# Two more weight subtractions on GpSimd for the last eight experts, and TensorE transposes for the last expert's tokens

## The chip, the cores and the metric

The kernel runs on one core of one Trainium2 chip. The metric is the device time of one execution in microseconds (us). Five engines work side by side on a core: TensorE (PE in the rows; PEld is its weight load), VectorE (DVE), ScalarE (ACT), GpSimd (POOL) and SyncE (SP), which here issues the weight loads. Each engine takes its own instructions in order, and they wait for one another through semaphores.

## The reference

Causal attention over 8 batches, 8 heads, 576 positions and 64 channels gives 4608 tokens of 512 values. A router then sends every token to one of 16 experts, and an expert is two matrix products:

```
for g in range(G):
    ...
    for e in range(Eg):
        ...
        h = np.maximum(xg[mask_e] @ w1[g, e], 0.0)
        ye = h @ w2[g, e]
        ...
        out[tok_idx] = combined[:, None] * ye
```

`w1` is 512 x 1024 and `w2` is 1024 x 512 for each expert, all in fp32.

## The kernel before

The first half of the time is attention and routing, which the change leaves alone. The second half (`moe`) works through 16 *slots*, one expert each, from the fullest to the emptiest; slot k takes up to `CAPS[k]` tokens, from 384 down to 256.

**Precision.** TensorE multiplies in a rounded fp32 form (`F32R`). Each operand is therefore split into a rounded high part and a low part, low = raw - high, and each product is done as high x high, high x low and low x high. Tokens give `xh`, `xl`; the hidden layer gives `hh`, `hl`; weights give `wh`, `wl`.

**Weights** (`Expert.load`, lines 970 to 1003). An expert has four blocks i = 0 to 3 (two halves of `w1`, two of `w2`), each 1 MB loaded by SP into one of three raw buffers, and each cut into four pieces j = 0 to 3 of 128 x 512. ScalarE casts every piece to its high part (line 991). The low part is made in one of two ways. For some pieces GpSimd subtracts (line 994). For the others ScalarE copies the piece a second time into a PSUM tile `pw` (line 999), and VectorE subtracts that from the raw piece (line 1000). The text below calls the pieces W0 to W15, piece W(4i+j) being piece j of block i. Before the change VectorE makes the low parts of W0, W4, W8, W10, W12 and W14, and GpSimd the ten others.

**Tokens** (`Slot.x_items`, lines 1034 to 1067). GpSimd gathers a slot's rows by indirect DMA (line 950). They must be turned so that channels lie on partitions. In slots 0 and 1 TensorE does that, with transposes into PSUM (line 1042), a ScalarE cast (1043) and a VectorE subtraction (1044) for each of four channel groups. In slots 2 to 15 VectorE does it with 32 stream transposes (line 1059) of 32 partitions each, 16 items of two; then ScalarE casts `xh` in two halves (1063) and VectorE subtracts `xl` in two halves (1064). With these widths the list holds eight transpose items of two and two split items, so a slot has 16 stream transposes.

**Products.** `h_items` makes the hidden layer in eight items of 12 matmuls (line 1092), each followed by a ScalarE Relu to `hh` (1087) and a VectorE `hl` (1088). `y_items` makes the second product in four items (line 1147, or line 1114 for the slots 14 and 15, whose `CAPS` is 256). For slots 1 to 13 the result comes out turned: ScalarE copies it to `yT` (1144, 1158), VectorE turns it back in 16 stream transposes during the *next* slot's hidden layer (1193), ScalarE scales the rows (1196), and GpSimd scatters them (955).

**Order** (lines 1407 to 1421). The order on TensorE, VectorE and ScalarE is written out by hand; GpSimd and SP are ordered by the planner. In slot k, after hidden item i come one item of the turning back of slot k-1 and weight piece W(i) of expert k+1. Ahead of second-product item i come four items of slot k+1's tokens, and weight pieces W(8+2i) and W(9+2i). Hence the eight transpose items run ahead of the first two second-product items, both splits ahead of the third, and the ScalarE queue after the splits is W12, W13, a `yT` copy, W14, W15, a `yT` copy, then the first Relu of slot k+1.

Of the kernel before, what the change touches and what calls it, by code (L numbers as in the profile page):

```python
# [24 lines left out]
E = 16  # L25
# [6 lines left out]

CAPS = [384, 368, 344, 332, 322, 314, 306, 300, 294, 288, 284, 280, 272, 264, 256, 256]
NL = 4
ROW = NTOK + P


# [16 lines left out]
def attn_moe(ctx, tc, qk, v, s, wr, w1, w2, out, stop_at=None, dbg=None):  # L54
# [8 lines left out]
    st.count = cst.tile([P, E], F32, name="count")  # L63
    st.lists = cst.tile([P, NV, E, NL], F32, name="lists")
    st.hot = cst.tile([P, B, NB, E], BF16, name="hot")
# [558 lines left out]
class Router:  # L624


    def __init__(self, tc, ac, sm, end, ps_t, ps_s, wr_f, wr_sb, xs, st):
# [25 lines left out]
        self.cols = iota("cols", [[1, P]])  # L653
        self.thr = iota("thr", [[P, NL + 1]])
        self.four = iota("four", [[1, NL]])
        self.lT = ac.tile([20, NB * P], F32, name="lT")
# [84 lines left out]
    def batch(self, b, xtail, xh, xl):  # L741
# [82 lines left out]
        place, us, pl = (small(i) for i in range(3))  # L824
        u4 = pc[:, 128:128 + NB * NL].rearrange("p (t h) -> p t h", h=NL)
        off = pc[:, 0:NB * E].rearrange("p (t e) -> p t e", e=E)
# [9 lines left out]

        U = [P, NB, NL]
        u = T("u", U[1:])
# [6 lines left out]
        yield  # L845
        col = T("col", [NB, E, NL], BF16)
        V.tensor_tensor(out=col, in0=ohb.unsqueeze(3).to_broadcast([P, NB, E, NL]),
# [73 lines left out]
def moe(tc, w1, w2, xs, st, out):  # L921
    nc = tc.nc
    V = nc.vector
    ident, mc = st.ident, st.cst
    with ExitStack() as ctx:
# [37 lines left out]
        class Expert:  # L963
# [6 lines left out]
            def load(self, hi=(None,) * 4, lo=(None,) * 4, eng=V):  # L970

                pieces = []

                with after(tc, *(loads[-1:] if 0 < self.u < E else ())):
                    e = nc.values_load(self.e, engines=[ENG.SP], min_val=0, max_val=E - 1)
                for i, w in enumerate((w1, w1, w2, w2)):

                    turn = 4 * self.u + i
                    q, n = (x1, 2) if turn % 3 < 2 else (x2, 1)
                    raw = q.tile([P, 4, 512], F32, name=f"raw{self.u}_{i}", tag="raw", bufs=n)  # L980
                    q, n = (wp, 4) if turn % 6 < 4 else (wq, 2)
                    h = q.tile([P, 4, 512], F32R, name=f"wh{self.u}_{i}", tag="wh", bufs=n)
                    l = q.tile([P, 4, 512], F32R, name=f"wl{self.u}_{i}", tag="wl", bufs=n)
                    self.h.append(h)
                    self.l.append(l)

                    def piece(j, i=i, w=w, raw=raw, h=h, l=l):
                        if j == 0:
                            loads.append(nc.sync.dma_start(raw, w[bass.ds(e, 1), i % 2].rearrange("o p a c -> p (o a) c")))
                        with after(tc, hi[i], lo[i]):  # L990
                            self.casts.append(nc.scalar.copy(h[:, j], raw[:, j]))  # L991

                            if j in ((1, 2, 3) if i < 2 else (1, 3)) or eng is not V:
                                self.low = nc.gpsimd.tensor_tensor(out=l[:, j], in0=raw[:, j],  # L994
                                                                   in1=h[:, j].bitcast(F32), op=ALU.subtract)
                                return

                            ps = pt.tile([P, 512], F32R, name=f"pw{self.u}_{i}_{j}", tag="pt")
                            nc.scalar.copy(ps, raw[:, j])
                            V.tensor_tensor(out=l[:, j], in0=raw[:, j], in1=ps.bitcast(F32), op=ALU.subtract)  # L1000

                    pieces += [lambda j=j, piece=piece: piece(j) for j in range(4)]
                return pieces
# [18 lines left out]
        class Slot:  # L1022
# [11 lines left out]
            def x_items(self):  # L1034
                u, cap = self.u, self.cap
                self.xh, self.xl = xhl(u, 0 if u == 0 else u + 1)

                def item(c):
                    q, tag = (pm[0], "pm") if u == 0 else (pt, "pt")
                    ps = q.tile([P, 512], F32, name=f"px{u}_{c}", tag=tag)  # L1040
                    for t, r in enumerate(self.rows):
                        nc.tensor.transpose(ps[:, t * P:t * P + r], self.xg[:r, t, c * P:(c + 1) * P], ident[:r, :r])
                    self.split = (nc.scalar.copy(self.xh[:, c, :cap], ps[:, :cap]),
                                  V.tensor_tensor(out=self.xl[:, c, :cap], in0=ps[:, :cap],
                                                  in1=self.xh[:, c, :cap].bitcast(F32), op=ALU.subtract))

                if u < 2:
                    return [lambda c=c: item(c) for c in range(4)]

                xt = turned(u)  # L1050
                nb = -(-cap // 32)

                def turn(j, i0):

                    n = len(range(j, nb, 4))
                    for i in (i0, i0 + 1):
                        src = self.xg[32 * j:32 * j + 32].rearrange("p t (c i n) -> p t c i n", c=4, n=32)
                        dst = xt[32 * i:32 * i + 32].rearrange("p c (t j n) -> p t c j n", j=4, n=32)
                        V.transpose(dst[:, 0:n, :, j], src[:, 0:n, :, i])  # L1059

                def split(a):
                    xh, xl, x = (t[:, a:a + 2, :cap] for t in (self.xh, self.xl, xt))
                    nc.scalar.copy(xh, x)  # L1063
                    V.tensor_tensor(out=xl, in0=x, in1=xh.bitcast(F32), op=ALU.subtract)  # L1064

                return ([lambda j=j, i=i: turn(j, i) for j in range(4) for i in (0, 2)] +
                        [lambda a=a: split(a) for a in (0, 2)])
# [191 lines left out]
        def run(items):  # L1259
            for f in items:  # L1260
                f()
# [15 lines left out]
        X = first.x_items()  # L1277
# [53 lines left out]
        with tc.manual_schedule(engines={ENG.PE}):  # L1331
# [10 lines left out]
            W = wts[1].load((first.rounded, rest.split[0], None, None), (None, rest.split[1], None, None))  # L1342
            run(W[:8])
            low = wts[1].low
            X, Z = slots[1].x_items(), first.z_items()
# [61 lines left out]
        Z = []  # L1407
        with tc.manual_schedule(engines={ENG.PE, ENG.DVE, ENG.Activation}):
            for k in range(1, E):
                W = wts[k + 1].load() if k + 1 < E else []  # L1410
                for i, f in enumerate(slots[k].h_items()):
                    f()
                    run(Z[i:i + 1] + W[i:i + 1])
                    if i == 4 and k + 2 < E:
                        slots[k + 2].gather()
                X = slots[k + 1].x_items() if k + 1 < E else []
                for i, f in enumerate(slots[k].y_items()):
                    run((Z[8:] if i == 0 else []) + X[4 * i:4 * i + 4] + W[8 + 2 * i:10 + 2 * i])
                    f()
                Z = slots[k].z_items()  # L1420
            run(Z)
# [164 lines left out]
```

## Time and profile before

| what | value |
|---|---|
| time, median of 3 runs | 954.95 us (954.18 to 956.15) |
| the profiled execution: its own time | 956.56 us |
| the profiled execution: span, first to last instruction | 954.8 us |
| PE busy | 875.1 us, 92% |
| DVE busy | 719.0 us, 75% |
| ACT busy | 615.3 us, 64% |
| POOL busy | 594.6 us, 62% |
| mean granted TensorE clock | 0.976 of full speed |

Times in the rows below are microseconds from the start of the span. A row of a timeline begins with the start and the duration; merged rows give the number of instructions as xN, and the bracket at the end is the idle time just before the row on that engine and what ended it. The shares of busy time are means over stages with different limits, so the stage that the change touches, from about 700 us to the end, is read by itself.

### The profile page before, as it was taken

The page shows a single profiled execution, that of the slowest core. Times are in us where ns is not written, and L with a number is a line of the kernel's source. Part 1 is how long each engine was busy: PE and PEld are TensorE (multiplying, and loading weights), DVE is VectorE, ACT ScalarE, POOL GpSimd, SP SyncE. Part 2 cuts the span into 40 slices and gives each one's busy share as a digit, 9 for nine tenths or more (in the row PEclk, how much of TensorE's full clock was granted, in tenths as well). Part 3 has the DMA queues.
Part 4 walks back from the last instruction along what each step waited for, and adds up shares of the span by engine and source line. Part 5 has one row for each costly group of instructions (what it writes and reads, how often), then busy time and mean ns, then how long its engine had stood idle before and what let it go on. Part 6 is the DMA issues. An engine that isn't in the chain of part 4 may idle for free. (4 is left out here: it accounts for less than half of the span.)

```text
span 954.8 us, 17985 instructions
## 1 busy us (share of the span) xinstructions
PE 875.1 (92%) x5640; PEld 785.2 (82%) x5640; DVE 719.0 (75%) x2032; ACT 615.3 (64%) x1396; POOL 594.6 (62%) x716
## 2 busy tenths in 40 slices
PE   4868999999999999998887999999999999999983
PEld 3657788887878788887686999999999999998882
DVE  7545586886868686876387578898888889988850
ACT  5546777776777677767634556667677666676640
POOL 9645666675757576534775447666676777676530
PEclk9999999999999999999898999999999999999987
DMA  6999988887888889723546345546555555565410
GB/s 184 217 182 207 240 217 214 194 224 197 222 197 224 210 213 231 174 69 112 194 142 211 130 160 189 186 162 225 182 204 187 201 194 176 209 221 210 143 42 22
DMA packets 80502, 174.66 MB, mean 183 GB/s; under 512 B 9580, under 2 KB 42988, under 8 KB 72208
## 3 DMA queue, kind: packets, MB, share of 16 engines
q1 hardware_dynamic: 70496, 153.52, 58.1%
q0 software_dynamic: 7488, 18.89, 5.6%
q10 hardware_dynamic: 2416, 1.03, 0.5%
q8 instruction: 47, 0.77, 0.3%
q14 instruction: 55, 0.45, 0.2%
HBM read 108.97 MB, written 19.69 MB: 135 GB/s over the span
## 5 line engine op out<-in xcount | busy, mean ns | idle before, releaser
L994 POOL TENSOR_TENSOR wl<-raw,wh 128x512 fp32r<-128x512 f32 x166 | 214.1, 1302 | 77.7 <-ACT wh L991 60.8
L221 DVE CUSTOM_DVE_ANT_0 mx<-pm,mask 128x192 bf16<-128x192 f32 (+4 forms) x320 | 129.4, 421 | 53.2 <-PE pm L213 49.0
L991 ACT CAST wh<-raw 128x512 fp32r<-128x512 f32 x256 | 155.2, 616 | 10.0 <-issue 9.4
L1092 PE MATMUL ph<-xh,wh 128*128 128x256 f32 (+13 forms) x512 | 145.9, 304 | 4.6 <-ACT xh L1063 3.9
L1092 PE MATMUL ph<-xl,wh 128*128 128x256 f32 (+13 forms) x512 | 146.4, 305 | 4.1 <-DVE xl L1064 3.8
L268 PE MATMUL ps<-WA 68*128 68x320 f32 (+4 forms) x384 | 136.9, 360 | 10.7 <-DMA WA<-tl 4.5
L213 PE MATMUL pm<-WA 66*128 66x288 f32 (+4 forms) x384 | 126.7, 359 | 17.6 <-DMA WA<-ch 10.3
L308 PE MATMUL po<-pt,VT 128*128 128x256 f32 (+3 forms) x512 | 123.2, 358 | 4.2 <-ACT sums L315 2.7
L1147 PE MATMUL py<-hl,wh 128*128 128x256 f32 (+13 forms) x448 | 113.6, 302 | 2.0 <-DVE hl L1088 2.0
L1147 PE MATMUL py<-hh,wh 128*128 128x256 f32 (+13 forms) x448 | 112.7, 301 | 0.0
L1059 DVE STREAM_TRANSPOSE xt<-xg 32x256 f32<-32x256 f32 (+1 forms) x224 | 109.5, 489 | 3.4
L270 PE MATMUL ps<-WB 128*128 128x320 f32 (+4 forms) x384 | 111.3, 303 | 0.0
L308 PE MATMUL po<-pu,VT 128*128 128x320 f32 (+1 forms) x384 | 107.8, 389 | 0.0
L1193 DVE STREAM_TRANSPOSE yr<-yT 32x384 f32<-32x384 f32 (+1 forms) x208 | 104.5, 502 | 4.2
L287 POOL TENSOR_SCALAR_AFFINE_SELECT pt<-pt 128x128 f32<-128x128 f32 (+2 forms) x192 | 63.9, 342 | 67.4 <-ACT pt L278 63.7
L1092 PEld LDWEIGHTS ph<-xl,wh 128*128 128x128 f32 x512 | 98.0, 191 | 7.8 <-DVE xl L1064 6.1
L1092 PEld LDWEIGHTS ph<-xh,wh 128*128 128x128 f32 x512 | 97.9, 191 | 7.2 <-ACT xh L1063 5.8
L308 PEld LDWEIGHTS po<-pt,VT 128*128 128x128 f32 x512 | 88.8, 195 | 18.1 <-issue 5.3
L213 PEld LDWEIGHTS pm<-WA 66*128 66x128 f32 (+1 forms) x384 | 69.8, 194 | 31.0 <-DVE mc L221 14.0
L370 POOL TENSOR_TENSOR xTl<-xT,xTh 128x512 fp32r<-128x512 f32 x30 | 38.2, 1273 | 90.6 <-ACT xTh L366 90.6
L1087 ACT ACTIVATE hh<-ph 128x256 fp32r<-128x256 f32 (+13 forms) x128 | 53.7, 420 | 62.7 <-PE ph L1092 61.9
L1092 PE MATMUL ph<-xh,wl 128*128 128x256 f32 (+13 forms) x512 | 90.8, 301 | 0.0
(245 smaller groups left out, 2017.5 us busy)
## 6 DMA issues: line engine op xcount, KB each, us to landing
raw<-in_w_dram SPq DMA_DIRECT2D x64, 1024.0 KB
r<-in_qk_dram SPq DMA_DIRECT2D x32, 576.0 KB
WA<-hl SPq DMA_DIRECT2D x61, 288.0 KB
WB<-hl SPq DMA_DIRECT2D x61, 288.0 KB
VT<-in_v_dram SPq DMA_DIRECT2D x32, 384.0 KB
WB<-hl SPq DMA_DIRECT2D x64, 144.0 KB
xs<-xr SPq DMA_DIRECT2D x15, 512.0 KB
WA<-cumd SPq DMA_DIRECT2D x56, 4.5 KB
```

The source lines that it names most:

```text
L213: nc.tensor.matmul(ps[:rows, :cw], WA[i][0:66, QA, h, QO + q0:QO + q0 + rows], WA[i][0:66, KA, h, QO + c0:QO + c0 + cw], start=True, stop= ...
L221: nc.vector.tensor_tensor_reduce(out=tmp[:rows, :cw], in0=ps[:rows, :cw], in1=mk[:rows], scale=1.0, scalar=-3.0e38 if c0 == 0 else mo, op0 ...
L268: nc.tensor.matmul(ps[:rows, o:o + w], WA[i][0:68, KA, h, QO + k0:QO + k0 + rows], WA[i][0:68, QA, h, QO + q0:QO + q0 + w], start=True, st ...
L270: nc.tensor.matmul(ps[:rows, o:o + w], WB[p % NBB][:, KA, h, k0:k0 + rows], WB[p % NBB][:, QA, h, q0:q0 + w], start=False, stop=True)
L287: nc.gpsimd.affine_select(out=d, in_=d, pattern=[[0, len(u)], [1, rows]], compare_op=ALU.is_ge, fill=0.0, base=0, channel_multiplier=-1)
L308: nc.tensor.matmul(po[0][:, qa - base:qb - base], VT[p % NVT].rearrange("p t a d -> p (t a d)")[:, (3 * t + 1 + h) * 64:][:, 0:P], x[:, c: ...
L991: self.casts.append(nc.scalar.copy(h[:, j], raw[:, j]))
L994: self.low = nc.gpsimd.tensor_tensor(out=l[:, j], in0=raw[:, j], in1=h[:, j].bitcast(F32), op=ALU.subtract)
L1059: V.transpose(dst[:, 0:n, :, j], src[:, 0:n, :, i])
L1092: self.product = nc.tensor.matmul(pss[f][:, :cap], w[f // 4][:, c, (f % 4) * P:(f % 4 + 1) * P], x[:, c, :cap], start=(c == 0 and w is sel ...
L1147: self.product = nc.tensor.matmul(pss[c][:, :cap], w[2 + f // 4][:, f % 4, c * P:(c + 1) * P], x[:, f, :cap], start=(f == 0 and w is self. ...
L1193: V.transpose(dst[:, 0:n, :, i], src[:, 0:n, :, j])
```

## The change

For experts 8 to 15 (`self.u >= LATE`), which are loaded during slots 7 to 14, the low parts of W10 and W14 are made by GpSimd instead of by the second ScalarE copy and the VectorE subtraction. For slot 15 the tokens are turned by TensorE as in slots 0 and 1: four items, each of two transposes, one cast and one subtraction, and one item stands ahead of each of slot 14's second-product items.

```
+LATE = 8
...
-                            if j in ((1, 2, 3) if i < 2 else (1, 3)) or eng is not V:
+                            if j in ((1, 2, 3) if i < 2 or self.u >= LATE else (1, 3)) or eng is not V:
                                 self.low = nc.gpsimd.tensor_tensor(out=l[:, j], in0=raw[:, j],
                                                                    in1=h[:, j].bitcast(F32), op=ALU.subtract)
                                 return
...
-                if u < 2:
+                if u < 2 or u == E - 1:
                     return [lambda c=c: item(c) for c in range(4)]
...
                 X = slots[k + 1].x_items() if k + 1 < E else []
+                n = 4 if len(X) > 4 else 1
                 for i, f in enumerate(slots[k].y_items()):
-                    run((Z[8:] if i == 0 else []) + X[4 * i:4 * i + 4] + W[8 + 2 * i:10 + 2 * i])
+                    run((Z[8:] if i == 0 else []) + X[n * i:n * i + n] + W[8 + 2 * i:10 + 2 * i])
                     f()
```

## Rows read from the trace of the kernel before

**Rows 1.** Busy time by stretch: length, busy us of each engine (instructions), clock, DMA.
```profile
858.00:884.00 26.00, 24.08 (x193) 23.39 (x193) 23.34 (x50) 17.99 (x40) 17.82 (x16) 1.00 0.56 202
...
900.00:920.00 20.00, 17.02 (x76) 14.49 (x76) 17.09 (x35) 10.61 (x21) 12.57 (x11) 0.83 0.21 83
```

**Rows 2.** Waits from 600 to 955 us: total us, times, longest us.
```profile
PE ph L1092 <- ACT xh L1063: 3.9, 5, 2.2
PE ph L1092 <- DVE xl L1064: 3.8, 9, 0.8
```

**Rows 3.** Waits of VectorE from 700 to 912.6 us.
```profile
DVE hl L1088 <- ACT hh L1087: 3.7, 8, 0.5
```

**Rows 4.** Timeline of VectorE in slots 13 and 14.
```profile
866.47 0.43 DVE L1088 SCALAR_TENSOR_TENSOR hl<-ph,hh 128x264 fp32r<-128x264 f32 x1 [0.44 <-ACT hh L1087]
...
884.77 2.25 DVE L1059 STREAM_TRANSPOSE xt<-xg 32x256 f32<-32x256 f32 x5
...
904.75 3.58 DVE L1059 STREAM_TRANSPOSE xt<-xg 32x256 f32<-32x256 f32 x8
```

**Rows 5.** Timeline of ScalarE: three late slots' token casts, and the queue behind them.
```profile
727.41 1.27 ACT L1063 CAST xh<-xt 128x588 fp32r<-128x588 f32 x2 [3.28 <-DVE xt L1059]
...
861.30 1.17 ACT L1063 CAST xh<-xt 128x528 fp32r<-128x528 f32 x2 [2.79 <-DVE xt L1059]
...
866.05 0.39 ACT L1087 ACTIVATE hh<-ph 128x264 fp32r<-128x264 f32 x1
...
887.04 1.14 ACT L1063 CAST xh<-xt 128x512 fp32r<-128x512 f32 x2 [2.26 <-DVE xt L1059]
...
890.44 0.58 ACT L999 CAST pw<-raw 128x512 fp32r<-128x512 f32 x1
890.96 0.62 ACT L991 CAST wh<-raw 128x512 fp32r<-128x512 f32 x1
...
912.67 1.14 ACT L1063 CAST xh<-xt 128x512 fp32r<-128x512 f32 x2 [2.80 <-DVE xt L1059]
```

**Rows 6.** Timeline of TensorE in slots 14 and 15.
```profile
887.72 0.39 PE L1092 MATMUL ph<-xh,wh 128*128 128x256 f32 x1 [0.36 <-ACT xh L1063]
...
900.05 0.40 PE L1114 MATMUL py<-wh,hh 128*128 128x512 f32 x1
...
910.73 0.39 PE L1114 MATMUL py<-wh,hl 128*128 128x512 f32 x1
913.35 0.58 PE L1092 MATMUL ph<-xh,wh 128*128 128x256 f32 x1 [2.23 <-ACT xh L1063]
...
927.11 0.28 PE L1092 MATMUL ph<-xh,wh 128*128 128x256 f32 x1
...
928.55 0.40 PE L1114 MATMUL py<-wh,hh 128*128 128x512 f32 x1
```

**Rows 7.** Instruction groups from 560 to 955 us: busy us, mean ns of one, idle before.
```profile
L994 POOL TENSOR_TENSOR wl<-raw,wh 128x512 fp32r<-128x512 f32 x130 | 167.2, 1296 | 60.1 <-ACT wh L991 43.8 <-issue 12.6 <-POOL wl L994 1.9
...
L1000 DVE TENSOR_TENSOR wl<-raw,pw 128x512 fp32r<-128x512 f32 x78 | 53.6, 687 | 17.9 <-ACT pw L999 14.1 <-issue 2.0
```

**Rows 8.** Timeline of TensorE at the transposes of slot 1, at full clock.
```profile
506.79 0.80 PE L1042 MATMUL px<-ident,xg 128*128 128x128 f32 x6
507.43 0.60 PE L1221 MATMUL prr<-ident,xg 128*128 128x128 f32 x4
```

**Rows 9.** A weight load: SP's issue, DMA by stretch (last two columns), ScalarE's first use.
```profile
887.85 10.42 SPq L989 DMA_DIRECT2D raw<-in_w_dram  x3
...
892.00:893.00 1.00, 1.00 (x11) 1.00 (x10) 0.83 (x2) 1.00 (x3) 0.96 (x1) 1.00 0.01 0
...
896.21 0.61 ACT L991 CAST wh<-raw 128x512 fp32r<-128x512 f32 x1
```

**Rows 10.** VectorE transposes and GpSimd subtractions at the same time, from the two timelines.
```profile
857.67 3.59 DVE L1059 STREAM_TRANSPOSE xt<-xg 32x256 f32<-32x256 f32 x8
...
857.46 2.56 POOL L994 TENSOR_TENSOR wl<-raw,wh 128x512 fp32r<-128x512 f32 x2
```

More of the change, by code (lines that the diff above doesn't have):

```diff
@@ L34 @@
 NL = 4
+LATE = 8
 ROW = NTOK + P
@@ L991, in piece @@
                             self.casts.append(nc.scalar.copy(h[:, j], raw[:, j]))
-                            if j in ((1, 2, 3) if i < 2 else (1, 3)) or eng is not V:
+                            if j in ((1, 2, 3) if i < 2 or self.u >= LATE else (1, 3)) or eng is not V:
                                 self.low = nc.gpsimd.tensor_tensor(out=l[:, j], in0=raw[:, j],
@@ L1045, in item @@
                                                   in1=self.xh[:, c, :cap].bitcast(F32), op=ALU.subtract))
-                if u < 2:
+                if u < 2 or u == E - 1:
                     return [lambda c=c: item(c) for c in range(4)]
@@ L1416, in moe @@
                 X = slots[k + 1].x_items() if k + 1 < E else []
+                n = 4 if len(X) > 4 else 1
                 for i, f in enumerate(slots[k].y_items()):
-                    run((Z[8:] if i == 0 else []) + X[4 * i:4 * i + 4] + W[8 + 2 * i:10 + 2 * i])
+                    run((Z[8:] if i == 0 else []) + X[n * i:n * i + n] + W[8 + 2 * i:10 + 2 * i])
                     f()
```

## The prediction, made before the changed kernel had run

> **What bounds the kernel now.** I read the busy time by stretch first. Late in the experts TensorE is busy 24.08 of 26 us at full clock, VectorE 23.34, ScalarE and GpSimd about 18 each; from 900 to 920 us TensorE falls to 17.02 and its granted clock to 0.83 [rows 1]. So two places cost TensorE time: a little in every late slot, and more at one boundary near the end. The waits name the releaser: TensorE's first hidden products wait for the token casts `xh` and subtractions `xl` [rows 2]. Both come out of the VectorE stream transposes, since each `xh` cast begins at an idle stretch that a transpose ended [rows 5].
>
> Who holds VectorE up? From 700 to 912.6 us it waits for a Relu 8 times, once in each of eight slots and 0.5 us at most [rows 3]. The timelines show the rest. In slot 13 the first `hl` starts at 866.47, and from there VectorE runs without a gap (hidden subtractions, turning back, three weight subtractions, 16 transposes) until the last transposes, five from 884.77 for 2.25 us, end at 887.02 [rows 4]. At 887.04 the `xh` cast starts [rows 5]. So a loop closes that does not contain TensorE: transposes end, ScalarE casts `xh` and works off its queue up to the first Relu, the first `hl` starts, VectorE runs solidly to the end of the next transposes. One turn, cast to cast: 861.30 to 866.05 on ScalarE (4.75), 0.42 to the first `hl` at 866.47, 20.57 on VectorE to 887.04; sum 25.74 [rows 4, 5]. TensorE starts slot 14 at 887.72, 0.68 after the cast [rows 5, 6]. TensorE's own need is smaller: a hidden item at full clock takes 928.55 - 927.11 = 1.44 us [rows 6], so eight take 11.52. The seven turns from the cast at 727.41 (slot 8) to the cast at 912.67 (slot 15) have this pattern, 26.5 us each on average [rows 5]. What shortens the loop moves the end by as much, as long as TensorE does not become the limit.
>
> The last boundary is the same loop with a larger penalty. Slot 14's second product begins at 900.05; its last matmul starts at 910.73 and the next instruction at 913.35, after 2.23 us of idling for `xh` [rows 6]. Behind that gap the granted clock is low (0.83 over 900 to 920 [rows 1]; it is 1.00 before), and slot 15's hidden layer takes 928.55 - 913.35 = 15.20 us instead of 11.52.
>
> **Part 1, W10 and W14 on GpSimd.** Removed in each of slots 7 to 14: two ScalarE copies into `pw` and two VectorE subtractions of 0.687 us; added: two GpSimd subtractions of 1.296 us [rows 7], 2.59 us a slot. What counts is which of the four removed instructions lies in the loop.
> - W14's ScalarE copy does: it stands between the `xh` cast and the next slot's first Relu, and the next cast starts 890.96 - 890.44 = 0.52 us behind it [rows 5]. Minus 0.52 us a turn.
> - W14's VectorE subtraction doesn't: it sits between the token splits and the first `hl`, where VectorE waits for ScalarE anyway [rows 3]. Zero; the Relu covers it, and without that cover it would have cost its 0.69.
> - W10's copy is queued before the `xh` cast, and ScalarE idles 2.26 to 3.28 us in front of that cast [rows 5]. Zero.
> - W10's VectorE subtraction stands behind the last transpose and ahead of the `xl` subtraction. `xl` must also wait for the first half of the cast (1.14 us for both, so about 0.6), nearly its 0.69. Taken as zero, at most 0.1 us a turn.
>
> TensorE does not stop this: in slot 14 it starts its first item at 887.72, and even with its start-up waits that item is over before the Relu, which ScalarE reaches 4.7 us after the cast. The turns of slots 8 to 13 carry the saving to TensorE's start of slot 14: 6 x 0.52 = 3.12 us, 884.60 instead of 887.72. Bounds for this part: 0 and 6 x 0.62 = 3.7.
>
> The 2.59 us on GpSimd: it is busy 17.82 of 26 us [rows 1], so 8.2 us are idle, and the addition leaves 20.4 of a turn of about 25.2. The first work that a late GpSimd would hurt is the weight load: a raw buffer is reloaded when its last subtraction is done. The load issued at 887.85 has landed by 892 (DMA 0.01 in 892 to 893) and is first cast at 896.21 [rows 9], so a lead of 4.2 us stands between a late subtraction and the loop. Also queued behind the two added subtractions are GpSimd's scatters and gathers; gathered rows are wanted a good half slot after their issue. Zero, and the rival below has the price if the idle time is not usable. Would the extra GpSimd work slow VectorE down? Eight transposes beside two running GpSimd subtractions take 3.59 us [rows 10]; eight at 904.75 take 3.58 [rows 4]. No.
>
> [...]
>
> **Part 2, slot 15's tokens on TensorE.** Removed from VectorE: 16 transposes (8 from 904.75 [rows 4], 8 more behind them, the last ending at the cast at 912.67 [rows 5]) and two wide splits. Added: 8 TensorE transposes in front of slot 14's four second-product items, four casts and four subtractions from PSUM. Transposes cost 507.43 - 506.79 = 0.64 us for six at full clock, 0.107 each [rows 8], 0.86 for eight; bounds 0.4 to 1.2. This is on TensorE's path and is paid.
>
> Slot 14 then: start 884.60; hidden layer 900.05 - 887.72 = 12.33 (its start-up waits stay); second product 910.73 - 900.05 and 0.23 for the last matmul (10.68 / 47) = 10.91; transposes 0.86. Slot 15 can start at 908.70.
>
> Are its operands there? ScalarE reaches them last. Its three row scalings of slot 13 wait for VectorE's turning back, which ends where the transposes began, 904.75 [rows 4], now 3.64 us earlier (seven turns up to slot 14's first Relu): 901.1. Then 1.9 us of scalings, and up to the fourth `xh` cast seven piece steps of 0.52 (W8 to W13 and one copy) and three token casts of about 0.3 (a 264-wide Relu from PSUM takes 0.39 [rows 5]): 901.1 + 1.9 + 3.6 + 0.9 = 907.5, done by 907.9, its `xl` by 908.4. The fourth channel group is wanted six matmuls into slot 15, at about 909.4. The cover is about 1 us; if it is gone, TensorE waits for the difference. The transposes themselves wait for gathered rows (gathered most of a slot earlier) and for a PSUM tile of four; the tightest is the fourth item, behind W8's VectorE subtraction, which ends near 905 while TensorE arrives near 905.7.
>
> With operands ready and no gap, the clock has no reason in these rows to fall, and slot 15's hidden layer takes 11.52: second product at 920.2 instead of 928.55. The rest, second product and scatters, is unchanged.
>
> **The sum.** 3.12 (loop) + (25.63 - 24.10 = 1.53: slot 14 start to slot 15 start) + (15.20 - 11.52 = 3.68) = 8.3 us. The profiled execution has a span of 954.8 and a time of 956.56, so about 946.5 and 948.2; the runs have a median of 954.95, which the profiled time exceeds by 1.6, and I take the same difference from it: 954.95 - 8.3 = 946.6.
>
> **Rivals.**
> 1. *The loop keeps its length.* Something else is late in ScalarE's or VectorE's queue behind the removed copy, for instance the first Relu waiting for TensorE. Against it: that Relu starts with no idle time before it at 866.05 [rows 5]. Only part 2 stays: 5.2 us, 949.7.
> 2. *The last boundary still stalls.* ScalarE gets to the fourth cast late; TensorE waits as long as now (2.4 us from slot 14's last matmul to slot 15) and slot 15 begins at the low clock. Then 3.68 and 2.4 are lost from the sum: 2.2 us left, 952.7. For it: the cover is only 1 us.
> 3. *GpSimd becomes the bound, and it is slower than before.* The 2.59 us find no usable idle time, because GpSimd's idle time is made of waits for ScalarE, TensorE rows and gathers that stay. Raw buffers then come free later by d every turn; the lead of 4.2 us is spent once and ScalarE waits for weights. It decides when 7d - 4.2 exceeds the 5.2 us of part 2, at d above 1.35 us of the 2.59. At the full 2.59: 954.95 + 18.1 - 4.2 - 5.2 = 963.7. Against it: 8.2 us of idle a turn [rows 1]. [...]
> 4. *It does nothing that can be measured*: VectorE or ScalarE give the time back elsewhere; about 955.
>
> **How the numbers follow.** Forecast 0.68, rival 1 0.12, rival 2 0.08, rival 3 0.06, rival 4 0.06. About 0.2%, 1.9 us, is what a measurement of this kernel can tell from no change. Faster: forecast, rival 1 and half of rival 2 (952.7 lies near the line), 0.84; same: the other half and rival 4, 0.10; slower 0.06. The forecast's own bounds: loop up to 0.6 us more, transposes 0.4 us to either side, the runs' spread about 1 us: 944.6 to 948.5. Rival 1 at 949.7 with the same spread gives the upper end, 950.6. Together 0.80.
>
> **What would show it.** In the changed trace: casts of slots 9 to 14 about 0.5 us closer each, slot 14 starting near 884.6; VectorE still without idle between first `hl` and last transpose; `pw` copies down by 16; no TensorE gap between slots 14 and 15 and a clock of 1.00 from 900 to 920 us; slot 15's hidden layer 11.5 us. I am wrong if the turns keep their 25.7 us, if ScalarE waits for a weight load, or if the gap at slot 15 returns.

## The result, and the profile after

The changed kernel took 942.66 us (median of 7 runs, 939.42 to 949.85), the kernel before 954.57 us beside it (7 runs, 951.75 to 956.84). The ratio is 0.9883, 95% interval 0.9849 to 0.9918. So it is faster, as forecast, but by 11.9 us instead of 8.3, and the median lies 1.9 us below the low end of the stated range. The profiled execution took 939.42 us, 17 us less than that of before. Four executions in the slow state (three of the kernel before, 958.85 to 960.37 us, and one of `again`, 958.41) are left out of all medians, means and ratios in this document.

Where did it gain? The page's busy line and, below it, busy time by stretch of the changed kernel (length, busy us of each engine with instructions, clock, DMA share, GB/s):

```profile
PE 867.3 (92%) x5648; PEld 779.6 (83%) x5648; DVE 702.2 (75%) x2002; ACT 608.3 (65%) x1382; POOL 615.0 (66%) x732
```

```profile
849.50:874.80 25.30, 24.01 (x192) 23.46 (x192) 21.78 (x47) 17.33 (x37) 20.03 (x17) 1.00 0.58 207
883.00:903.00 20.00, 20.00 (x126) 17.89 (x125) 13.43 (x29) 13.10 (x29) 15.22 (x14) 1.00 0.37 142
```

A late slot now lasts 25.3 us, and GpSimd is busy 20.03 of them. TensorE has no idle time over the last boundary (883 to 903 us) and its clock is 1.00 there; before it was busy 17.02 of 20 us at 0.83 [rows 1].

The timeline of TensorE in slots 14 and 15 of the changed kernel (start, length, engine and line, operation, idle time before it and who ended it); lines are one higher than before:

```profile
875.50 0.38 PE L1093 MATMUL ph<-xh,wh 128*128 128x256 f32 x1 [0.41 <-ACT xh L1064]
...
887.83 0.38 PE L1043 MATMUL px<-ident,xg 128*128 128x128 f32 x2
...
896.73 0.38 PE L1043 MATMUL px<-ident,xg 128*128 128x128 f32 x2
...
899.70 0.28 PE L1093 MATMUL ph<-xh,wh 128*128 128x256 f32 x1
...
911.21 0.40 PE L1115 MATMUL py<-wh,hh 128*128 128x512 f32 x1
```

The four transpose items start without idle time, slot 15 follows slot 14 after 24.20 us (25.63 before [rows 6]), and its hidden layer takes 911.21 - 899.70 = 11.51 us (15.20 before).

The loop shows on ScalarE and VectorE in slot 13 (cast, first Relu, first `hl`, last transposes, next cast; the rows of two timelines):

```profile
849.55 1.17 ACT L1064 CAST xh<-xt 128x528 fp32r<-128x528 f32 x2 [3.35 <-DVE xt L1060]
...
853.78 0.40 ACT L1088 ACTIVATE hh<-ph 128x264 fp32r<-128x264 f32 x1
...
874.83 1.14 ACT L1064 CAST xh<-xt 128x512 fp32r<-128x512 f32 x2 [2.82 <-DVE xt L1060]
```

```profile
854.21 0.43 DVE L1089 SCALAR_TENSOR_TENSOR hl<-ph,hh 128x264 fp32r<-128x264 f32 x1 [1.71 <-ACT hh L1088]
...
871.20 3.59 DVE L1060 STREAM_TRANSPOSE xt<-xg 32x256 f32<-32x256 f32 x8
```

Cast to first Relu is 4.23 us (4.75 before), first `hl` to next cast 20.62 (20.57 before), the turn 25.28 (25.74 before) [rows 4, 5].

Now the surprise. The table gives the stages as TensorE's timelines show them, with the experiments told below. P2 is the start of slot 2's hidden layer, P8, P14 and P15 those of slots 8, 14 and 15; h15 is slot 15's hidden layer; "late part" runs from P2 to the last matmul. What comes ahead of P2 is attention, the gate and slots 0 and 1. All in us; ratios are to the kernel before, measured beside it, with n runs.

| kernel | median (n) | ratio, 95% | P2 | P8-P2 | P14-P8 | P15-P14 | h15 | late part |
|---|---|---|---|---|---|---|---|---|
| before | 954.57 (7) | 1 | 557.47 | 170.68 | 159.57 | 25.63 | 15.20 | 381.76 |
| after | 942.66 (7) | 0.9883 (0.9849-0.9918) | 548.03 | 170.73 | 156.74 | 24.20 | 11.51 | 373.86 |
| control | 953.21 (12) | 1.0014 (0.998-1.0049) | 557.55 | 170.67 | 159.56 | 25.64 | 15.45 | 382.00 |
| again | 945.88 (11) | 0.9938 (0.9913-0.9964) | 554.31 | 170.69 | 156.66 | 24.32 | 11.51 | 373.86 |
| part1 | 948.33 (12) | 0.995 (0.992-0.998) | 556.43 | 170.72 | 156.71 | 25.16 | 12.34 | 375.61 |
| part2 | 949.93 (12) | 0.9974 (0.9947-1.0) | 549.36 | 170.69 | 159.62 | 25.86 | 11.52 | 378.37 |
| w14 | 944.11 (1) | | 551.85 | 170.66 | 156.46 | 25.32 | 11.51 | 374.63 |
| w10 | 957.09 (1) | | 562.37 | 170.71 | 159.78 | 24.31 | 11.52 | 377.00 |
| all2 | 942.6 (8) | 0.9894 (0.9858-0.993) | 552.59 | 169.41 | 156.10 | 24.31 | 11.52 | 372.02 |
| w8 | 950.66 (12) | 0.9971 (0.9944-0.9997) | 561.32 | 170.58 | 159.27 | 26.41 | 11.52 | 378.46 |
| w12late | 946.54 (6) | 0.9923 (0.9894-0.9952) | 559.34 | 170.67 | 153.39 | 24.21 | 11.51 | 370.46 |
| w12all | 940.47 (4) | 0.9859 (0.9823-0.9894) | 555.38 | 169.25 | 152.30 | 24.25 | 11.51 | 367.99 |
| w8w12 | 940.96 (4) | 0.9871 (0.9828-0.9914) | 557.42 | 169.26 | 150.16 | 25.57 | 11.52 | 367.19 |

The change gained 381.76 - 373.86 = 7.90 us in the late part. The other 9.4 us between the two first traces lie ahead of P2 (557.47 against 548.03), where both kernels have the same instructions in the same order on every engine. The two traces part early; busy time by stretch, first of before, then of after:

```profile
20.00:40.00 20.00, 16.52 (x64) 13.12 (x63) 11.72 (x46) 7.56 (x18) 11.67 (x18) 1.00 0.94 227
40.00:60.00 20.00, 15.06 (x77) 12.46 (x78) 8.55 (x35) 11.03 (x27) 13.69 (x19) 0.91 1.05 196
60.00:80.00 20.00, 14.99 (x81) 12.45 (x80) 9.58 (x34) 9.67 (x24) 7.98 (x13) 0.91 1.07 182
```

```profile
20.00:40.00 20.00, 16.76 (x72) 13.48 (x73) 12.54 (x50) 9.26 (x23) 13.34 (x19) 1.00 0.94 249
40.00:60.00 20.00, 17.23 (x82) 13.96 (x80) 9.67 (x36) 9.55 (x22) 12.96 (x18) 0.83 1.04 213
60.00:80.00 20.00, 17.02 (x106) 14.72 (x106) 11.63 (x44) 15.77 (x40) 11.24 (x17) 1.00 0.99 217
```

In both, the transfer engines are as good as full (share 0.94 to 1.07), but over the 60 us they move 202 GB/s on average in before, (227 + 196 + 182) / 3, and 226 in after, (249 + 213 + 217) / 3. The same VectorE instruction, its 200th, starts at 95.22 us in before and at 88.34 in after, so 6.9 of the 9.4 us are there by then; the rest comes later, where the share is lower. That the transfers set the pace is read off their share and no run tried it; TensorE's granted clock differs in these rows too (0.91 and 0.91 against 0.83 and 1.00). Is the difference the change, or chance? The first two experiments ask that.

### The profile page after: what moved, and what is told of

It is laid out like the page before. It is cut to its first block, busy times and chain, and to the rows that moved or that the text cites. A ratio compares the mean times of both kernels' runs of the same rounds, so it can differ in the third digit from the quotient of the medians.

```text
span 937.7 us, 17973 instructions
## 1 busy us (share of the span) xinstructions
PE 867.3 (92%) x5648; PEld 779.6 (83%) x5648; DVE 702.2 (75%) x2002; ACT 608.3 (65%) x1382; POOL 615.0 (66%) x732
## 5 line engine op out<-in xcount | busy, mean ns | idle before, releaser
L995 POOL TENSOR_TENSOR wl<-raw,wh 128x512 fp32r<-128x512 f32 x182 | 233.5, 1303 | 63.7 <-ACT wh L992 48.1
L1060 DVE STREAM_TRANSPOSE xt<-xg 32x256 f32<-32x256 f32 (+1 forms) x208 | 102.5, 493 | 3.2
L156 POOL TENSOR_TENSOR WB<-r,hl 64x576 fp32r<-64x576 f32 x62 | 87.2, 1406 | 5.3 <-DMA WB<-hl 2.4
```

Source lines behind the costliest of these rows:

```text
L156: (nc.vector if p < 1 else nc.gpsimd).tensor_tensor(out=hl[:, 2] if part else WB[p % NBB][0:64, KA, h], in0=r[hr, part], in1=hl[hr, part]. ...
```

## The experiments

### Both kernels once more: again and control

`again` is the changed kernel and `control` the kernel before, each unaltered. Theory A: the early difference is the spread of the stage with the full transfer engines and has nothing to do with the change. Theory B: the changed program itself makes that stage faster.

> The changed kernel once more. Theory A (the change saves 7.9 us, all of it behind slot 7; whatever more was measured comes from the attention stage, whose length varies from execution to execution in either kernel): from the start of slot 2's hidden layer to the last matmul 373.9 us as in the first trace of the changed kernel (381.8 before), while the start of slot 2 itself may lie anywhere from 546 to 560 us; median ratio to the kernel before near 0.9917. Theory B (the changed program also makes the attention stage faster, though its instruction order there is the same): slot 2 starts near 548 us again, and the ratio stays near 0.988.

> The kernel before once more, as a control. Both theories: 381.8 us from slot 2's start to the last matmul, and ratio 1.000 within its interval. Theory A: the start of slot 2 differs from the 557.5 us of the first trace by several us, either way. Theory B: it is again within a microsecond or two of 557.5.

Measured: `again` repeats the late part to 0.01 us (373.86) and starts slot 2 at 554.31 instead of 548.03, with the same instructions. `control` has a late part of 382.00 and starts at 557.55. The rows in which slot 2 begins, of after, again and control:

```profile
548.03 0.32 PE L1093 MATMUL ph<-xh,wh 128*128 128x344 f32 x1
```

```profile
554.31 0.32 PE L1093 MATMUL ph<-xh,wh 128*128 128x344 f32 x1
```

```profile
557.55 0.32 PE L1092 MATMUL ph<-xh,wh 128*128 128x344 f32 x1
```

So the same kernel moves by 6.3 us there, and the first trace of after was an early one. Over all these runs, the kernel before has 81 times (those of `control` among them) with a mean of 953.0 and a standard deviation of 3.1, the changed one 18 times with 944.8 and 3.1: a difference of 8.2 us, 95% interval 6.6 to 9.8, on 7.9 of the late part. Theory A fits this pair; what is left over for theory B is 0.3 us, with 1.6 either way. What lets the transfers run faster in one execution than in the next no run here shows.

### Each part alone: part1 and part2

`part1` keeps the two low parts on GpSimd and turns slot 15's tokens on VectorE as before:

```
-                if u < 2 or u == E - 1:
+                if u < 2:
```

> Only the weight subtractions are moved (W10 and W14 of experts 8 to 15 on GpSimd); slot 15's tokens are turned by VectorE as before. Loop theory: each of the seven turns from slot 8 to slot 15 is 0.46 to 0.48 us shorter, 3.3 us at slot 15's start, and the last boundary keeps its idle stretch of about 2.2 us and the low clock, so slot 2's start to the last matmul takes 378.4 us. Rival (the saving counts only together with the TensorE transposes, because the last boundary is the only bound): 381.8. Rival (GpSimd is the bound): above 381.8. Theory A puts the median ratio near 0.9965, theory B near 0.988 less what part 2 gives.

`part2` turns slot 15's tokens on TensorE and leaves the low parts of W10 and W14 where they were:

```
-                            if j in ((1, 2, 3) if i < 2 or self.u >= LATE else (1, 3)) or eng is not V:
+                            if j in ((1, 2, 3) if i < 2 else (1, 3)) or eng is not V:
```

> Only slot 15's tokens are turned by TensorE; all weight pieces are made as before. Loop theory: turns of 27.25 to 25.6 us as before, slot 14 starts as before; the idle stretch ahead of slot 15 and the low clock behind it go, worth 1.4 plus 3.7 us; ScalarE has one more copy ahead of the fourth token cast (W10's pw), so up to 0.4 us of it comes back as a wait: 376.7 to 377.1 us from slot 2's start to the last matmul. Rival (the boundary stalls all the same, since ScalarE is late with the fourth cast): 380 or more.

The gain of the loop belongs to part 1 alone: P14-P8 is 156.71 in `part1` and 159.62 in `part2` (159.57 before). But `part1` ends 2.8 us earlier than expected (375.61 against 378.4), because slot 15's hidden layer took 12.34 us, not 15.2. TensorE still idles before it, less long. Its row in `part1`, and the clock around it (the last but two column):

```profile
909.02 0.39 PE L1093 MATMUL ph<-xh,wh 128*128 128x256 f32 x1 [1.75 <-ACT xh L1064]
```

```profile
907.00:909.00 2.00, 0.27 (x2) 0.00 (x0) 1.94 (x4) 0.66 (x2) 1.74 (x2) 1.00 0.00 0
909.00:911.00 2.00, 1.64 (x10) 1.38 (x11) 1.71 (x4) 2.00 (x5) 1.20 (x1) 1.00 0.00 0
911.00:913.00 2.00, 2.00 (x19) 2.00 (x18) 1.36 (x3) 1.46 (x5) 1.80 (x2) 1.00 0.34 131
```

The same place in before, where the idle time was 2.23 us [rows 6]:

```profile
911.00:913.00 2.00, 0.12 (x1) 0.00 (x0) 1.93 (x5) 0.33 (x1) 0.86 (x1) 1.00 0.00 0
913.00:915.00 2.00, 0.90 (x2) 0.61 (x3) 2.00 (x4) 2.00 (x5) 0.70 (x1) 0.58 0.00 0
915.00:919.00 4.00, 4.00 (x20) 4.00 (x20) 2.60 (x5) 2.31 (x5) 3.63 (x4) 0.50 0.17 66
```

After 2.23 us of idling the clock went to half for the 4 us from 915 (0.50); after 1.75 us it stayed at 1.00. So either part alone saves the clock here (slot 15's hidden layer takes 12.34 us in `part1` and 11.52 in `part2`, 15.20 before): 381.76 - 375.61 = 6.15 us for part 1 and 3.39 for part 2, 9.5 together where both at once give 7.9.

`part2` ends later than expected too (378.37 against 376.7 to 377.1), for a reason on TensorE. Its transpose items at the end of slot 14:

```profile
895.02 0.38 PE L1043 MATMUL px<-ident,xg 128*128 128x128 f32 x2
899.50 0.44 PE L1043 MATMUL px<-ident,xg 128*128 128x128 f32 x2 [1.34 <-DVE xl L1045]
902.55 0.38 PE L1043 MATMUL px<-ident,xg 128*128 128x128 f32 x2
```

One item waits 1.34 us until VectorE has read an earlier `px` tile. The four PSUM tiles of this rotation also serve `pw`: with W8 and W10 among the takers, the third item gets the first item's tile back. In the whole change W10 needs no `pw`, and the wait is gone. The two parts help each other here, which the prediction had not seen.

### Which of the two low parts does what: w14 and w10

Both have part 2. `w14` moves only W14 to GpSimd, `w10` only W10:

```
+ (w14) if j in ((1, 2, 3) if i < 2 or (self.u >= LATE and i == 3) else (1, 3)) or eng is not V:
+ (w10) if j in ((1, 2, 3) if i < 2 or (self.u >= LATE and i == 2) else (1, 3)) or eng is not V:
```

> The changed kernel, but only W14 is moved to GpSimd; W10 keeps its ScalarE copy into PSUM and its VectorE subtraction. Loop theory: W14's copy is the piece in the loop, so the turns of slots 8 to 13 are as short as in the changed kernel (26.8 to 25.3 us, 156.7 us from slot 8's to slot 14's start). PSUM theory for the last boundary: W10's PSUM tile is back in the rotation of four, so slot 15's third transpose item must wait for the first item's VectorE subtraction and slot 14 to slot 15 takes about 25.5 us, not 24.2. Rival (W10's VectorE subtraction, behind the last transposes, is what shortens the turn): 159.6 us from slot 8 to slot 14.

> The changed kernel, but only W10 is moved; W14 stays on ScalarE and VectorE. Loop theory: turns as in the kernel before, 159.6 us from slot 8's to slot 14's start. PSUM theory: no wait for a PSUM tile at the third transpose item, slot 14 to slot 15 in 24.2 to 24.4 us and no low clock. Rival (W10 shortens the turn): 156.7 to 158.

One run each, so with the spread seen above only the stages count, and they answer plainly: `w14` has the loop's gain (156.46) and the wait at the boundary (P15-P14 25.32), `w10` has neither (159.78 and 24.31). In the waits of TensorE from 880 to 910 us, `w14` still has the PSUM wait:

```profile
PE px L1043 <- DVE xl L1045: 0.8, 1, 0.8
```

`w10` has no such line. So the loop's gain goes by W14, and W10's use is the tile that it gives back. Both of W14's instructions, the copy and the VectorE subtraction, leave together in `w14`; that it is the copy is seen in the turn, where ScalarE's part alone became shorter (4.75 to 4.23 us in slot 13, above). W10 also costs something: with it (after) the loop takes 156.74, without it (`w14`) 156.46, about 0.05 us in every turn. On balance it is worth 374.63 - 373.86 = 0.77 us.

### Earlier slots too: all2

```
-LATE = 8
+LATE = 2
```

> The changed kernel with W10 and W14 on GpSimd for experts 2 to 15 instead of 8 to 15. Loop theory: the six turns of slots 2 to 7 also become 0.47 us shorter, so slot 8's token casts come 2.8 us earlier; TensorE can use it only as far as it waited: slot 2 to slot 8 170.7 minus 1.4 us (the start-up waits of slots 6 and 7 go), and the rest of the 2.8 us is kept as a lead that the following slots use up, so slot 2's start to the last matmul is 373.9 - 2.8 = 371.1 us. Rival (GpSimd is the bound in the fuller slots, with three gathers and three scatters a slot): 373.9 or more. Rival (the early slots are TensorE-bound and the lead is lost by slot 8): 373.9.

Measured 372.02, 0.9 us more than expected: the six early turns give 170.73 - 169.41 = 1.3 us, about as expected, but of the lead that was to be kept the late slots show only 156.74 - 156.10 = 0.6 us. Time 942.6 us (8 runs).

### One more piece for GpSimd: w8

```
-                            if j in ((1, 2, 3) if i < 2 or self.u >= LATE else (1, 3)) or eng is not V:
+                            if j in ((0, 1, 2, 3) if self.u >= LATE and i == 2 else (1, 2, 3) if i < 2 or self.u >= LATE else (1, 3)) or eng is not V:
```

W8's low part goes to GpSimd as well, 13 pieces an expert. It takes another 0.7 us off VectorE's solid run; the rival says that GpSimd becomes the bound.

> The changed kernel with W8 moved to GpSimd too, for experts 8 to 15: GpSimd makes 13 low parts a slot. W8's VectorE subtraction lies between the two groups of transposes, inside the loop: each turn should be 0.70 us shorter still (26.78 to 26.08 in slot 8, 25.3 to 24.6 in slot 13), unless TensorE is the limit. TensorE's own need with its start-up waits is about 26.5, 26.2, 26.5, 25.4, 24.9 and 23.9 us in slots 8 to 13, so it becomes the limit in the first three and about 2.5 us are left of 4.2: 154.2 us from slot 8 to slot 14, and 371.3 us from slot 2's start to the last matmul. Rival (GpSimd is the bound): its 13 subtractions, three scatters and three gathers come to about 16.9 + 3.9 + 4.5 = 25.3 us with their issue gaps, so turns of 25.3 us or more in slots 11 to 13, weight loads later, ScalarE waiting for raw pieces; 373.9 us or more.

It lost 4.6 us against after (378.46), but not because ScalarE waited for weights: its casts have no idle time before them (group from 560 to 953 us, last column):

```profile
L992 ACT CAST wh<-raw 128x512 fp32r<-128x512 f32 x209 | 126.1, 614 | 0.0
```

TensorE's waits from 690 to 930 us, first `w8`, then after:

```profile
PE ph L1093 <- DVE xl L1065: 9.8, 9, 1.9
```

```profile
PE ph L1093 <- DVE xl L1065: 3.6, 7, 1.0
```

TensorE waits for VectorE's token subtraction `xl`. The timelines of VectorE and GpSimd of `w8` in slot 10 show why (both `xl` instructions, and the last two of four GpSimd subtractions that follow one another from 783.37):

```profile
785.70 3.29 DVE L1065 TENSOR_TENSOR xl<-xt,xh 128x568 fp32r<-128x568 f32 x1 [0.73 <-ACT xh L1064]
...
788.91 0.74 DVE L1065 TENSOR_TENSOR xl<-xt,xh 128x568 fp32r<-128x568 f32 x1
```

```profile
785.87 1.28 POOL L995 TENSOR_TENSOR wl<-raw,wh 128x512 fp32r<-128x512 f32 x1
787.12 1.25 POOL L995 TENSOR_TENSOR wl<-raw,wh 128x512 fp32r<-128x512 f32 x1
```

The first `xl` takes 3.29 us instead of 0.75. It ends at 788.99, 0.62 after GpSimd's last subtraction (787.12 + 1.25 = 788.37), and the second, with GpSimd done, takes 0.74. GpSimd's two take 1.28 and 1.25 us, against a mean of 1.296 before [rows 7]. So here `xl` outlasts GpSimd's subtractions, and GpSimd loses nothing. It is not always so: the second `xl` of slot 14 in `w8` gets in between two GpSimd subtractions, and the one behind it takes 1.73 us instead of about 1.27 (`xl`, then that subtraction):

```profile
892.74 1.80 DVE L1065 TENSOR_TENSOR xl<-xt,xh 128x512 fp32r<-128x512 f32 x1
```

```profile
893.96 1.73 POOL L995 TENSOR_TENSOR wl<-raw,wh 128x512 fp32r<-128x512 f32 x1
```

With `xl` so late, TensorE is back in the loop: in slot 10 it idles 1.91 us for `xl`, and ScalarE's first Relu then waits 1.58 us for TensorE. The clock adds to it. TensorE's row behind the idle time, and the clock from 789 us:

```profile
789.05 0.40 PE L1093 MATMUL ph<-xl,wh 128*128 128x284 f32 x1 [1.91 <-DVE xl L1065]
```

```profile
789.00:791.00 2.00, 1.95 (x13) 1.85 (x14) 1.25 (x2) 0.43 (x2) 1.70 (x2) 0.94 0.72 197
791.00:793.00 2.00, 2.00 (x10) 2.00 (x10) 1.50 (x4) 1.41 (x3) 1.97 (x3) 0.50 0.98 410
793.00:795.00 2.00, 2.00 (x13) 2.00 (x12) 1.42 (x3) 0.92 (x2) 2.00 (x3) 0.71 0.45 180
```

By these rows the lower clock costs slot 10 an estimated (0.06 + 0.50 + 0.29) x 2 = 1.7 us, so not all of the 4.6 us is waiting for `xl`.

The slowing of `xl` is in the change itself too, smaller. The groups of that shape from 600 to 930 us, of before, after and `w14`:

```profile
L1064 DVE TENSOR_TENSOR xl<-xt,xh 128x568 fp32r<-128x568 f32 x2 | 1.4, 748 | 0.0
```

```profile
L1065 DVE TENSOR_TENSOR xl<-xt,xh 128x568 fp32r<-128x568 f32 x2 | 2.0, 1026 | 0.7 <-ACT xh L1064 0.7
```

```profile
L1065 DVE TENSOR_TENSOR xl<-xt,xh 128x568 fp32r<-128x568 f32 x2 | 1.4, 747 | 0.0
```

W10's subtraction is queued on GpSimd just where `xl` begins; with W10 left on VectorE (`w14`) `xl` is back at 747 ns.

### Moving pieces where `xl` isn't hurt: w12late, w12all, w8w12

If the GpSimd subtraction at the same time is the cause, W12 (queued behind `xl`) can go to GpSimd, and W10 comes back to VectorE. `w12late` does it for experts 8 to 14, `w12all` for 2 to 14. `w8w12` also puts W8 on GpSimd and gives it W9 but not W10 and W11:

```
+ (w12late) if j in (((1, 2, 3), (1, 2, 3), (1, 3), (0, 1, 2, 3))[i] if LATE <= self.u < E - 1 else
+                    (1, 2, 3) if i < 2 or self.u >= LATE else (1, 3)) or eng is not V:
+ (w12all)  ... if 2 <= self.u < E - 1 else ...
+ (w8w12)   ... (0, 1) as third entry, if 2 <= self.u < E - 1 else ...
```

> From the changed kernel, for experts 8 to 14 another choice of 12 pieces for GpSimd: all four of the last block (W12 to W15), and in the third block only W9 and W11, so that W10 goes back to ScalarE and VectorE; expert 15 as in the changed kernel. Loop theory: both copies W12 and W14 had stood in ScalarE's queue between the token casts and the first Relu, so the turns of slots 8 to 13 become another 0.52 us shorter (26.2, 26.1, 25.5, 25.5, 25.3, 24.7), 153.4 us from slot 8's to slot 14's start instead of 156.7, and 370.7 us from slot 2's start to the last matmul. Sharing theory (a GpSimd subtraction that runs at the same time holds back VectorE's xl subtraction, which reads two SBUF tensors): W10 no longer runs just ahead of xl, so the xl subtractions of slots 9 to 11 take 0.74 to 0.76 us each again, not 0.9 to 1.0. Rival (12 subtractions are GpSimd's limit wherever they stand): 373.9 or more.

> The same choice for experts 2 to 14. Loop theory: six more turns become 1.04 us shorter, a lead of 6.2 us at slot 8, which TensorE cannot follow fully; it is then the limit in nearly all slots: 169.5 us from slot 2 to slot 8 (170.7 before) and 148 to 150 us from slot 8 to slot 14, 364 to 366 us from slot 2's start to the last matmul. Rival (GpSimd, with three scatters and three gathers in the fuller slots, falls behind and meets xl): 370 or more.

> As the one before, but in the third block GpSimd makes W8 and W9, and ScalarE and VectorE make W10 and W11; still 12 pieces for GpSimd. Loop theory alone: W8's VectorE subtraction leaves the loop, W11's joins W10's between the last transposes and xl, outside it: turns another 0.7 us shorter, TensorE the limit everywhere, but each slot's first low products wait 0.7 us longer where no lead is left; 363 to 365 us. Rival: two VectorE subtractions ahead of xl delay each slot's start by about 0.7 us, 366 to 369 us.

`w12late` came out as expected: late part 370.46, P14-P8 153.39, and `xl` at 748 ns again:

```profile
L1066 DVE TENSOR_TENSOR xl<-xt,xh 128x568 fp32r<-128x568 f32 x2 | 1.4, 748 | 0.0
```

`w12all` gained in the early slots as expected (169.25) but took 152.3 in the late ones, so 367.99 instead of 364 to 366: a lead of the loop can't grow past the point where ScalarE's first Relu waits for TensorE. In after it waits for nothing in slots 3 to 5; in `w12all` it waits 0.98, 0.36 and 0.68 us. The row of slot 3:

```profile
587.75 0.45 ACT L1089 ACTIVATE hh<-ph 128x332 fp32r<-128x332 f32 x1 [0.98 <-PE ph L1094]
```

`w8w12` has the shortest loop (150.16) but not the 363 to 365 us of the loop theory: its 367.19 lies in the rival's range of 366 to 369. In slot 14 (25.57 against 24.25 in `w12all`) TensorE waits 0.62 and 0.95 us for `xl`, the second of them beside a GpSimd subtraction (1.77 us instead of 0.69).

By time `w12all` (940.47 us, ratio 0.9859, 0.9823 to 0.9894) and `w8w12` (940.96) lead and can't be told apart; the ratios of after were 0.9883 and 0.9938. The interval of `w12all` overlaps that of the first of these; what separates it from after is the late part, 5.87 us shorter. One thing doesn't fit: `w12late` should gain 11.3 us by its late part, and its six runs (943.71 to 948.11) gain 6.2 at the median. Its traced slot 2 begins at 559.34. Time less late part is 571.3 us in the mean of the kernel before and 575.9 for `w12late`; with a standard deviation of 3.1, six runs seldom lie 4.6 us off by chance. So an effect of that program on the early stage isn't ruled out, and theory A is not shown beyond the pair that was run again.

## Why the prediction was right, and where it was wrong

- **Bound and loop: right.** TensorE's start-up in the late slots goes by a loop of ScalarE and VectorE; W14's copy is the one of the four removed instructions in it. 0.52 us a turn was forecast, 159.57 - 156.74 = 2.83, or 0.47 a turn, was measured: 0.52 off ScalarE's part of slot 13's turn, and 0.05 more on VectorE's. `w14` and `w10` show that it is W14, and ScalarE's part of the turn that it is its copy. The three zeros hold as terms of the loop: VectorE's wait for the first Relu grew from 0.44 [rows 4] to 1.71 us, so W14's subtraction was under that cover; ScalarE's idle time ahead of the cast grew from 2.79 [rows 5] to 3.35, so W10's copy was in idle time; and `w10` without W14 has no gain in the loop.
- **The load on GpSimd: right in size.** Forecast 20.4 busy of 25.2 us, measured 20.03 of 25.3, and ScalarE's weight casts from 560 to 938 us have no idle time before them (the last column of this group):

```profile
L992 ACT CAST wh<-raw 128x512 fp32r<-128x512 f32 x203 | 123.4, 616 | 0.0
```

  Rival 3 didn't come. `w8` is one piece further and the gain of the loop is gone (159.27), but by `xl` (3.29 us instead of 0.75 in slot 10) and the lower clock behind it (0.50), not by raw buffers coming free late.
- **"Would the extra GpSimd work slow VectorE down? No.": wrong as a step, harmless in the sum.** It was judged by the transposes alone [rows 10], and these hardly change (8 in 3.59 us also in after). The two-input `xl` was not looked at; it goes from 748 to 1026 ns for 128x568, with a TensorE wait of 1.0 us at the longest in one slot. `xl` isn't in the loop, so a slot that starts late by it is followed by a shorter one (slots 10 and 11: 27.04 and 25.06 us in after, 26.48 and 25.54 in `w14`). The 156.74 - 156.46 = 0.3 us by which after is behind `w14` are not `xl`: slots 12 and 13, whose `xl` keep their time (720 and 704 ns), lose the same 0.05 us. They are in VectorE's run up to the last transposes; why, no run shows.
- **The last boundary: right.** Slot 14's hidden layer 12.33 us (forecast 12.33), second product with transposes 899.70 - 887.83 = 11.87 (11.77), slot 15's hidden layer 11.51 (11.52). P15-P14 fell by 1.43 (1.53). The cover of about 1 us was there: `xl` of the fourth channel group (row below) ends at 899.68, and its first matmul starts at 900.53, 0.85 us later. Rival 2 didn't come.

The timeline of VectorE and of TensorE of after at that point:

```profile
899.26 0.42 DVE L1045 TENSOR_TENSOR xl<-px,xh 128x256 fp32r<-128x256 f32 x1
```

```profile
900.53 0.28 PE L1093 MATMUL ph<-xl,wh 128*128 128x256 f32 x1
```

- **The tightest transpose item: half right.** The wait for a PSUM tile was named, with a cover of 0.7 us, for the fourth item. It isn't there in the change, and it was there for the third item in `part2` (1.34 us) and in `w14` (0.8).
- **Who earns what: not as told.** Rival 1 priced part 2 alone at 5.2 us; `part2` gained 3.39, with a TensorE wait of 1.34 us for a PSUM tile that W10's `pw` brings about. Part 1's term was 3.12, and `part1` gained 6.15, since behind 1.75 us of idling the clock stayed at 1.00. W10 was given no gain, and with its tile given back it is worth 0.77 us net. That 9.5 us of the parts make 7.9 in the whole was not foreseen.
- **The sum: right.** 8.3 us forecast (3.12, 1.53 and 3.68); 7.90 by the traces (2.83, 1.43 and 3.69, less 0.05 in slots 2 to 7), 8.2 (6.6 to 9.8) by the mean over all runs.
- **The step that failed: "the runs' spread about 1 us".** It was read off three runs that lay within 2 us (954.18 to 956.15). The 81 runs of that kernel spread over 943.5 to 959.9, standard deviation 3.1, and the interval of the measured ratio reaches 0.35% to either side, not the 0.2% that the prediction allowed. Both ends of the sum suffered. The 954.95 that it started from lies 1.9 us above the mean of the 81 runs, and the 942.66 of the first seven runs lies 2.1 us below the mean of 18 runs of the changed kernel (944.8). From 953.0 the same 8.3 us would have led to 944.7. The first seven of after had a mean of 943.4, the next eleven 945.7: 2.3 us apart, 3.0 either way, which chance can do; no run shows another cause. An estimate from the spread: a median of seven is uncertain by 1.25 x 3.1 / sqrt(7) = 1.5 us and one of three by 2.2, together 2.7; with twice that in place of 1 us the low end belonged near 941, not 944.6. (On the other side the terms named give 948.0, not 948.5.) The prediction looked only at the experts; nothing in it asked how firmly the 557 us ahead of them stand, though the transfer engines are full early there, as the rows of 20 to 80 us above show.

## What to carry to other kernels

Look for the closed loop of waits, and price a moved instruction by whether it lies in it. Before giving a range, ask how firm the stages are that the change doesn't touch: a stage can move by more than the edit from one execution to the next (here 6.3 us in a stage that begins with full transfer engines, share 0.94 to 1.07), and a trace that is compared stage by stage shows the edit to some tenths of a microsecond all the same. When work goes to GpSimd, look at what VectorE runs at the same time, and place it beside what kept its time here: the transposes (3.59 us for eight) and the subtractions with one input in PSUM (0.69 us each).

## What the runs showed of the hardware

In `w8`, `xl`, a VectorE subtraction of two SBUF tensors, took 3.29 us instead of 0.75 beside GpSimd's subtractions of two SBUF tensors, and ended 0.62 us after the last of them. In slot 10 it ended behind all that GpSimd had in a row; in slot 14 it got in between, and GpSimd's next one took longer (1.73 us). VectorE's transposes kept their time: eight took 3.59 us in after from 871.20, with GpSimd subtracting from 871.44 to 875.24. So did its subtractions with one input in PSUM (`wl` 687 ns in after, 687 before [rows 7]): at least 17 of those in after run for at least 0.6 us beside a GpSimd subtraction, and each took 0.69 us. Their group in after, from 550 to 940 us:

```profile
L1001 DVE TENSOR_TENSOR wl<-raw,pw 128x512 fp32r<-128x512 f32 x62 | 42.6, 687 | 10.0 <-ACT pw L1000 7.3 <-issue 1.1
```

Which of the two went first was not the same each time. In slot 10 of `w8`, `xl` began at 785.70 and ended behind the two GpSimd subtractions that began after it, at 785.87 and 787.12. In slot 14 of `w8` it went ahead: `xl` began at 892.74 and ended at 894.54, ahead of the GpSimd subtraction that began at 893.96 and ended at 895.69. What makes the difference, and why their times grow beside each other, no run here shows.

The granted clock stayed at 1.00 when TensorE had idled 1.75 us (`part1`) and fell to 0.50 when it had idled 2.23 us (before), at the same boundary. Slot 15's hidden layer took 12.34 us in the one and 15.20 in the other, 2.9 us more. In `w8` it fell to 0.50 behind 1.91 us of idling (slot 10). But in before the clock also stayed at 1.00 behind 2.69 us of idling that ended at 64.70 (the rows below), so the length of the idle time alone doesn't settle it, and no run varied it by itself. These are single traces of each kernel.

```profile
64.70 0.67 PE L308 MATMUL po<-pt,VT 128*128 128x256 f32 x2 [2.69 <-ACT sums L315]
```

```profile
64.70:67.00 2.30, 2.30 (x16) 2.20 (x17) 0.91 (x4) 2.21 (x6) 0.23 (x1) 1.00 1.01 195
67.00:70.00 3.00, 3.00 (x21) 2.68 (x21) 2.57 (x10) 2.94 (x9) 2.10 (x4) 1.00 1.02 163
```
